# Where the two operands of a matmul begin: stationary tiles at 64 bytes, moving tiles at 192

## The chip, the cores and the metric

One core of a Trainium2 chip runs the kernel. The metric is the device time of one launch in microseconds, as the median of several runs. Lower is better.

## The reference

The input is q, k and v of 8 batches, 8 heads, 576 rows and a head size of 64. Each head computes a linear attention, its rows are normalized, and the result, as 4,608 rows of 512, passes through two dense layers with a GELU between them.

```python
kv = np.einsum('bhsd,bhse->bhde', k, v)
out = np.einsum('bhsd,bhde->bhse', q, kv)
rms = np.sqrt(np.mean(out * out, axis=-1, keepdims=True) + 1e-06)
x = (out / rms * g_norm)         # then transposed and reshaped to 4608 x 512
h = x @ w_in                     # 512 -> 2048
g = 0.5 * h * (1.0 + erf(h * inv_sqrt2))
return (g @ w_out)               # 2048 -> 512
```

## The kernel before

The 4,608 rows are cut into nine chunks of 512. The first two chunks (`PLAIN`) run both dense layers as plain matmuls (L665 for layer 1, L692 for layer 2, 512 columns each), while the other engines form sums of weight blocks and store them in DRAM. The other seven chunks, from `FAST` on, run each layer as seven block products instead of eight. These seven chunks are where the change is.

Every value is split into a high and a low part, and a product of two values is made of three matmuls: high with high, low with high, high with low. A matmul has a stationary operand, which is loaded into the array first (LDWEIGHTS, in the profile PEld), and a moving one, which then streams through. In these seven chunks each matmul has 128 stationary columns and 256 moving ones.

- Layer 1 (`product`, matmul at L554): the weights are stationary and the pieces of x are moving. It goes over eight parts j, each with seven products. A product of one key pair is six matmuls; two products share one place of weights, so twelve matmuls read the same place. The halves of the parts are interleaved by `parts_of_layer1`. Three matmuls per k block go through stationary high, low, high.
- Layer 2 (`Fast.matmuls`, matmul at L1241): the activations are stationary (`op`) and the weights are moving (`w`). It goes over 28 ticks (`TICKS`), of twelve matmuls each. The stationary operand goes high, high, low.

Between the parts of layer 1 stand other matmuls of the next chunk: the projections of q (L241), the fold of the sums of squares (L293) and the sums of keys and values (L188).

The weights come from DRAM in transfers of 512 KB through a ring of six places (`RING`, filled by `fetch`, released by `used`), or stay in SBUF for good (`keep` for four of layer 1; `kept_half` for nine of layer 2). A place is a tile of 4,096 bytes in each partition; those of the ring and of the kept weights have 256 bytes more (`EXTRA`), so that what lies in them may begin a little behind their start. `LINE` is 16 elements (64 bytes) and `AWAY` is three of them (192 bytes).

Before the change, all weights that come through the ring begin at `AWAY`, except those that `aligned` names, which begin at the place's start: the first of layer 2's ticks in each chunk, and three or four products of layer 1 in each chunk. In the first six chunks these follow a change of what TensorE works on (another layer, or L241, L293 or L188); in the last chunk three of them stand between other products of layer 1. The kept weights of both layers begin at `AWAY`. The other operand of each of these matmuls (pieces of x in layer 1, activations in layer 2) begins at a place's start.

The order of the instructions is that of the code; the pools hold every tile at a fixed place.

Of the kernel before, what the change touches and what calls it, by code (L numbers as in the profile page):

```python
# [9 lines left out]
F32R = mybir.dt.float32r  # L10
# [13 lines left out]
FAST = PLAIN  # L24
# [13 lines left out]
def linear_attn_rms_gelu_ffn(  # L38
# [18 lines left out]
    NT, DM = out.shape  # L57
    B, NP = kv_main.shape[:2]
# [5 lines left out]
    NCH = NT // CH  # L64
# [27 lines left out]
    LINE = 16  # L92
    AWAY = 3 * LINE
    KEPT_IN = [f"w_out{i}" for i in (4, 5, 6, 7)]
# [9 lines left out]
    def block_tile(name, dtype):  # L104
        return const.tile([P, 2 * DM + EXTRA.get(name, 0)], dtype, name=name)
# [69 lines left out]
    def rows(r):  # L175
        return slice(r * D, (r + 1) * D)
# [209 lines left out]
    kept = {}  # L386

    def reused(i, dtype=F32):

        if i not in kept:  # L390
            kept[i] = block_tile(f"w_in{i}", dtype)
        return kept[i][:, :2 * DM]
# [77 lines left out]
    TICKS = [(0, 0), (0, 1), (0, 2), (2, 0), (2, 1), (0, 3), (2, 2), (2, 3)]  # L470
# [19 lines left out]
    resident = {}  # L490
    queue = []
# [5 lines left out]
    ring = {}  # L497

    def fetch(n):

        if n < len(queue):
            key = queue[n][1]
            i = RING[n % len(RING)]
            reused(i, F32R)
            away = 0 if aligned(*queue[n]) else AWAY
            ring[n] = kept[i][:, away:away + 2 * DM]
            nc.sync.dma_start(out=ring[n].bitcast(F32), in_=products[key])

    def aligned(c, key):

        kind, j, k = key
        if kind == "out":
            return (j, k) == TICKS[0]
        if k:
            return False
        if c > FAST and c + 1 < NCH:
            return j in ((0, 1, 4, 7) if c + 2 < B else (0, 1, 4))
        return j in (0, 2, 3, 4)

    def operand(c, key):  # L520
        at = c, key
# [2 lines left out]
    def used(c, key):  # L524
        if (c, key) in place:
            n = place[c, key]
            ring.pop(n)
            fetch(n + len(RING))
# [5 lines left out]
        return name, block_tile(name, dtype)[:, :2 * DM]  # L534

    def keep(key):
        t = resident[key] = block_tile(KEPT_IN[key[1]], F32R)[:, AWAY:AWAY + 2 * DM]
        nc.sync.dma_start(out=t.bitcast(F32), in_=products[key])

    SETS = (("h0", "h1"), ("acc0", "acc1"), ("acc2", "acc3"))  # L540
# [242 lines left out]
    for d in range(0, 2 * D, BLK):  # L783
        h = d // D * D
        nc.gpsimd.tensor_tensor(
            out=fold[:, d:d + BLK], in0=ident[:, h:h + BLK], in1=ident[:, h + BLK:h + 2 * BLK],
# [24 lines left out]
    def column(n, t):  # L811
        return n_fold + 2 * ((n - 2) * NG + t)

    def sum_squares(n):
# [12 lines left out]
        out=half_g, in0=ps[:, :1], scalar1=0.5, scalar2=None, op0=ALU.mult  # L827
# [3 lines left out]
        out=sums[:, :P], lhsT=ones, rhs=eps, start=True, stop=False,  # L831
# [4 lines left out]
        out=root_g, in0=half_g, scalar1=D ** 0.5, scalar2=None, op0=ALU.mult  # L836
# [9 lines left out]
    for half in range(2):  # L846
# [6 lines left out]
        out=sums[:, :n_fold].rearrange("p (g b) -> p g b", g=2), lhsT=fold,  # L853
# [3 lines left out]
    for half in range(2):  # L857
        nc.scalar.activation(
            out=first.block((1, half)),
# [8 lines left out]
    for half in range(2):  # L868
# [3 lines left out]
            out=first.o_all[:, half], in0=first.ps.pop((0, half)), scalar=root_g, in1=bc,  # L872
            op0=ALU.mult, op1=ALU.mult,
        )
        n = 2 + half
        bc = bank(f"acc{n}")
        for t in range(NG):
            for h in range(2):
                at = column(n, t) + h
                nc.tensor.matmul(  # L880
                    out=bc[rows(h), t * P:(t + 1) * P],
# [173 lines left out]
    def later(c, i):  # L1055

        if i == 7:
            sums[c] = attn[c + 1].fold()
        if i in (5, 7):
            load_kv(c + 2, (i - 5) // 2)  # L1060
        if i == 9:
            attn[c + 2].load(0)
        if i == 10:
            attn[c + 2].load(1)
        if i in (5, 7):
            raw_out(6 + i // 7)
        if i == 15:
            place_kv(c + 2, range(NP))
        send()
        for n in {9: (0, 1), 14: (2, 3), 15: (4, 5)}.get(i, ()):  # L1070
            fetch(n)
        for n in {6: (0,), 9: (1,), 12: (2,), 14: (3,)}.get(i, ()):
            keep(RESIDENT[n])
# [43 lines left out]
    for s in range(PLAIN * NF):  # L1117
        c, i = divmod(s, NF)
# [5 lines left out]
        if c == 0:  # L1124
# [25 lines left out]
            for _ in range(2):  # L1150
                if i > 6 and RAW:
                    store_raw, j = RAW.pop(0)
# [8 lines left out]
        else:  # L1161
            spread_matmuls(c, i)
            g[s] = gelu(h.pop(s))
            nxt, k = attn[c + 1], SQUARES.index(i) if i in SQUARES else None
# [189 lines left out]
    for c in range(FAST, NCH):  # L1354
        at = attn[c]
# [3 lines left out]
        for j, second in parts_of_layer1():  # L1359
# [26 lines left out]
            if waiting and (last or (j, second) != (waiting[0], True)):  # L1386
                n = waiting.pop(0) // 2
# [65 lines left out]
```

## Time and profile before

| What | Value |
|---|---|
| Median of 3 runs | 775.71 us (775.59 to 778.14) |
| Span of the profiled execution | 774.5 us |
| What the two shortest runs lie above that span | 1.1 to 1.2 us |
| TensorE matmul (PE) busy | 767.6 us, 99% |
| TensorE weight load (PEld) busy | 726.5 us, 94% |
| VectorE (DVE) busy | 578.8 us, 75% |
| ScalarE (ACT) busy | 360.4 us, 47% |
| GpSimd (POOL) busy | 157.7 us, 20% |
| Packets of the main DMA queue | 87.9% of 16 engines' span |
| Mean granted TensorE clock | 0.999 |

The profile is of one execution, and its own time is given only as the span from the first to the last instruction; the time of a run also holds what lies around that. In the timeline a row is a number of like instructions in a row: its start, the time until the modelled end of the last one, the engine, the line, the operation, what it writes and reads, and how many there are. Matmuls overlap each other, so a row's own length is longer than what it adds; the start of one row to the start of the next is what the instructions took. Tile names are those of the places, which are used over and over: a piece of x can lie in a place called `w_in` or `s`.

### The profile page before, as it was taken

The page shows a single profiled execution, that of the slowest core. Times are in us where ns is not written, and L with a number is a line of the kernel's source. Part 1 is how long each engine was busy: PE and PEld are TensorE (multiplying, and loading weights), DVE is VectorE, ACT ScalarE, POOL GpSimd, SP SyncE. Part 2 cuts the span into 40 slices and gives each one's busy share as a digit, 9 for nine tenths or more (in the row PEclk, how much of TensorE's full clock was granted, in tenths as well). Part 3 has the DMA queues.
Part 4 walks back from the last instruction along what each step waited for, and adds up shares of the span by engine and source line. Part 5 has one row for each costly group of instructions (what it writes and reads, how often), then busy time and mean ns, then how long its engine had stood idle before and what let it go on. Part 6 is the DMA issues. An engine that isn't in the chain of part 4 may idle for free.

```text
span 774.5 us, 16764 instructions
## 1 busy us (share of the span) xinstructions
PE 767.6 (99%) x6598; PEld 726.5 (94%) x6598; DVE 578.8 (75%) x1057; ACT 360.4 (47%) x689; POOL 157.7 (20%) x141
## 2 busy tenths in 40 slices
PE   8999999999999999999999999999999999999998
PEld 6888888888899999999999999999999999999998
DVE  3999987899668974789477947694689568964683
ACT  3777645534363644364334724462436353632460
POOL 1000145423527000610043002500160016001100
PEclk9999999999999999999999999999999999999999
DMA  9997966797999999979998999989898989799974
GB/s 343 406 408 255 334 227 227 241 357 263 337 312 353 374 339 348 372 266 353 349 356 298 320 376 332 335 276 346 306 328 281 346 302 325 243 329 339 331 244 168
DMA packets 89602, 244.89 MB, mean 316 GB/s; under 512 B 8884, under 2 KB 30900, under 8 KB 89524
## 3 DMA queue, kind: packets, MB, share of 16 engines
q1 hardware_dynamic: 89520, 243.83, 87.9%
q8 instruction: 52, 0.85, 0.4%
q14 instruction: 26, 0.21, 0.1%
q10 hardware_dynamic: 4, 0.00, 0.0%
HBM read 207.09 MB, written 34.08 MB: 311 GB/s over the span
## 4 chain that ended last, share of the span: by engine, by line
PE 95%; DMA 2%; DVE 2%; ACT 0%; SPq 0%; issue 0%
PE acc L1241 23%; PE acc L554 22%; PE h L554 13%; PE acc L692 11%; PE h L665 11%; PE a L1241 10%; PE a L188 2%; PE a L241 1%; DMA kv_main<-kv_main 1%; PE h L655 1%; DMA w_in<-qT 1%; PE acc L241 1%; DVE x L1219 1%; PE acc L880 0%; PE a L293 0%; DVE x L1208 0%
## 5 line engine op out<-in xcount | busy, mean ns | idle before, releaser
L665 PE MATMUL h<-x,w_in 128*128 128x512 f32 x360 | 87.0, 390 | 0.0
L665 PEld LDWEIGHTS h<-x,w_in 128*128 128x128 f32 x360 | 67.3, 188 | 14.4 <-ACT w_in L641 0.3
L692 PE MATMUL acc<-w_out,gh 128*128 128x512 f32 x256 | 79.6, 392 | 0.0
L554 PE MATMUL acc<-w_in,w_in 128*128 128x256 f32 x480 | 64.7, 278 | 0.0
L554 PEld LDWEIGHTS acc<-w_in,w_in 128*128 128x128 f32 x480 | 59.1, 188 | 0.3 <-issue 0.2
L692 PEld LDWEIGHTS acc<-w_out,gh 128*128 128x128 f32 x256 | 47.5, 188 | 10.2 <-issue 0.3
L554 PE MATMUL acc<-x,w_in 128*128 128x256 f32 x390 | 52.8, 279 | 0.0
L545 DVE TENSOR_TENSOR gl<-acc,gh 128x256 f32<-128x256 f32 (+1 forms) x77 | 34.4, 446 | 24.2 <-ACT gh L567 18.5
L692 PE MATMUL acc<-w_out,gl 128*128 128x512 f32 x128 | 49.8, 389 | 0.0
L554 PEld LDWEIGHTS acc<-x,w_in 128*128 128x128 f32 x390 | 48.1, 188 | 1.0 <-issue 0.8
L678 ACT ACTIVATE gh<-h 128x512 fp32r<-128x512 f32 x32 | 19.2, 599 | 63.0 <-PE h L665 63.0
L1241 PE MATMUL acc<-w_in,w_in 128*128 128x256 f32 x372 | 46.7, 277 | 0.0
L567 ACT COPY gh<-h 128x256 f32<-128x256 f32 x21 | 7.8, 369 | 81.7 <-PE h L554 81.7
L1241 PEld LDWEIGHTS acc<-w_in,w_in 128*128 128x128 f32 x372 | 44.4, 188 | 0.0
L1208 POOL TENSOR_TENSOR w_in<-w_in,w_in 128x512 f32<-128x512 f32 x5 | 6.5, 1298 | 181.5 <-ACT w_in L586 181.5
L1241 PE MATMUL acc<-w_in,x 128*128 128x256 f32 x324 | 40.6, 277 | 0.0
L334 POOL TENSOR_TENSOR o<-o,sq 128x512 f32<-128x512 f32 x24 | 33.3, 1386 | 35.2 <-DVE sq L338 34.3
L586 ACT ACTIVATE w_in<-acc 128x512 f32<-128x512 f32 x32 | 19.2, 599 | 44.0 <-DVE acc L545 44.0
L554 PE MATMUL h<-w_in,w_in 128*128 128x256 f32 x288 | 38.7, 277 | 0.0
L1241 PEld LDWEIGHTS acc<-w_in,x 128*128 128x128 f32 x324 | 38.6, 188 | 0.1
L283 DVE TRANSPOSE_TENSOR_REDUCE part<-sq 128x16 f32<-128x512 f32 x33 | 23.4, 708 | 17.1 <-ACT sq L273 17.1
L554 PEld LDWEIGHTS h<-w_in,w_in 128*128 128x128 f32 x288 | 35.5, 188 | 0.0
(302 smaller groups left out, 1911.2 us busy)
## 6 DMA issues: line engine op xcount, KB each, us to landing
w_in<-products_in SPq DMA_DIRECT2D x168, 512.0 KB, 5.3
w_in<-products_out SPq DMA_DIRECT2D x133, 512.0 KB, 5.1
products_in<-w_in SPq DMA_DIRECT2D x40, 256.0 KB, 3.9
w_in<-w_in SPq DMA_DIRECT2D x16, 512.0 KB, 10.2
kv_main<-kv_main SPq DMA_DIRECT2D x16, 512.0 KB, 6.4
w_out<-w_out SPq DMA_DIRECT2D x16, 512.0 KB, 10.2
q<-qT SPq DMA_DIRECT2D x15, 512.0 KB, 6.5
products_out<-w_out SPq DMA_DIRECT2D x23, 256.0 KB, 3.9
```

Source lines behind the costliest of these rows:

```text
L188: nc.tensor.matmul(out=ps[r, n * D:(n + 1) * D], lhsT=k[:, r], rhs=v[:, r], start=(j == 0), stop=(j == NJ),)
L241: nc.tensor.matmul(out=ps[rows(h), p % 2 * HALF + a:p % 2 * HALF + e], lhsT=kv[b % 2][rows(half), p, h ^ half], rhs=q[rows(half), h, a:e], ...
L283: nc.vector.tensor_reduce(out=self.part[:, 2 * k[0] + k[1], :], in_=sq.rearrange("p (b d) -> p b d", d=BLK), op=ALU.add, axis=AX.X, apply_ ...
L334: eng.tensor_tensor(out=o, in0=o, in1=bc, op=ALU.mult)
L545: return eng.tensor_tensor(out=out, in0=x, in1=y, op=op)
L554: nc.tensor.matmul(out=out, lhsT=y, rhs=x[:, z, kb], start=first and kb + i == 0, stop=kb == 1 and i == 2, skip_group_check=True,)
L567: nc.scalar.copy(out=u[:, left], in_=a[:, left])
L586: nc.scalar.activation(out=grid(t)[:, :, j % 2], in_=ps.rearrange("p (a n) -> p a n", a=2), func=AF.Gelu)
L665: nc.tensor.matmul(out=h, lhsT=parts["in", i][:, w][:, p * P:(p + 1) * P], rhs=at.x[p][:, x], start=(m + p == 0), stop=(m == 2 and p == NP ...
L678: nc.scalar.activation(out=gh, in_=h, func=AF.Gelu)
L692: nc.tensor.matmul(out=ps, lhsT=x[:, ts], rhs=parts["out", i][:, w], start=(i == 0 and m == 0), stop=(m == 2 and (i == NF - 1 or (i, t) == ...
L1241: nc.tensor.matmul(out=self.bank[name][a][:, a * HALF:(a + 1) * HALF], lhsT=x[:, at], rhs=y, start=(k in (0, 2, 1) and n + p + m == 0 and ...
```

## The change

The weights of layer 1 now begin at `LINE`, 64 bytes into their places, both those of the ring and the four that are kept. The weights of layer 2 begin at `AWAY`, 192 bytes, all of them. The function `aligned` and its list are gone. No instruction is added, removed or moved, and the instructions, their order and their waits are the same on every engine; only starting addresses of operands in these places differ (of 2,436 matmuls and 179 transfers).

```diff
             i = RING[n % len(RING)]
             reused(i, F32R)
-            away = 0 if aligned(*queue[n]) else AWAY
-            ring[n] = kept[i][:, away:away + 2 * DM]
+            at = LINE if key[0] == "in" else AWAY
+            ring[n] = kept[i][:, at:at + 2 * DM]
             nc.sync.dma_start(out=ring[n].bitcast(F32), in_=products[key])
-
-    def aligned(c, key):
-
-        kind, j, k = key
-        if kind == "out":
-            return (j, k) == TICKS[0]
-        if k:
-            return False
-        if c > FAST and c + 1 < NCH:
-            return j in ((0, 1, 4, 7) if c + 2 < B else (0, 1, 4))
-        return j in (0, 2, 3, 4)
...
     def keep(key):
-        t = resident[key] = block_tile(KEPT_IN[key[1]], F32R)[:, AWAY:AWAY + 2 * DM]
+        t = resident[key] = block_tile(KEPT_IN[key[1]], F32R)[:, LINE:LINE + 2 * DM]
         nc.sync.dma_start(out=t.bitcast(F32), in_=products[key])
```

## The prediction

> **What bounds the kernel now.** I read the page's totals and its chain first, then the waits of PE, and then the timeline of PE, where the cost of a starting byte shows.
>
> ```profile
> span 774.5 us, 16764 instructions
> PE 767.6 (99%) x6598; PEld 726.5 (94%) x6598; DVE 578.8 (75%) x1057; ACT 360.4 (47%) x689; POOL 157.7 (20%) x141
> PEclk9999999999999999999999999999999999999999
> PE 95%; DMA 2%; DVE 2%; ACT 0%; SPq 0%; issue 0%
> ```
>
> PE is busy all the time, carries 95% of the chain that ended last, and has its full clock in every slice. The waits of PE, all there are that end at DMA or at another engine:
>
> ```profile
> PE a L188 <- DMA kv_main<-kv_main: 1.2, 2, 0.8
> PE h L772 <- DVE w_in L741: 1.1, 1, 1.1
> PE a L188 <- DMA w_out<-kv_main: 0.5, 2, 0.3
> PE h L818 <- ACT gl L807: 0.4, 1, 0.4
> PE acc L241 <- ACT kv L199: 0.3, 1, 0.3
> PE acc L1241 <- DVE x L1219: 0.2, 1, 0.2
> ```
>
> They are 3.7 us in all, and in the two lines that the change touches (L554 for layer 1, L1241 for layer 2) there is one, of 0.2 us. So time is lost or won only by the spacing of PE's own matmuls, and the busy times of the page, which are unions, don't show that. The timeline does: each product is 12 matmuls (6 where two products share half a place), and from one row's start to the next is what they took.
>
> I name a product by its two remainders modulo 256 bytes, counted from the start of a place (all places start alike, since each is 4,096 or 4,352 bytes and the built program puts them end to end; steps within an operand are multiples of 512 bytes). "Distance" is that of the moving operand minus that of the stationary one, in bytes. Before, layer 1 has +64 (moving 0, stationary 192), layer 2 has -64 (moving 192, stationary 0), and the products listed by `aligned` have 0. First the change from layer 1 to layer 2 in the first chunk of seven products: 250.31 is layer 1 at +64, 250.99 is the first tick of layer 2 at 0, the rest layer 2 at -64.
>
> ```profile
> 250.31 0.84 PE L554 MATMUL acc<-w_in,w_out 128*128 128x256 f32 x6
> 250.99 1.60 PE L1241 MATMUL acc<-w_in,w_in 128*128 128x256 f32 x12
> 252.43 1.54 PE L1241 MATMUL acc<-w_in,s 128*128 128x256 f32 x12
> 253.81 1.52 PE L1241 MATMUL acc<-r,x 128*128 128x256 f32 x12
> 255.17 2.88 PE L1241 MATMUL acc<-w_in,x 128*128 128x256 f32 x24
> ...
> 261.26 1.42 PE L1241 MATMUL acc<-w_out,x 128*128 128x256 f32 x10 [0.22 <-DVE x L1219]
> ```
>
> At +64 six matmuls take 0.68 (113 ns each). At distance 0 twelve take 1.44 (120 ns each). The next twelve, at -64, take 1.38, and then every twelve take 1.36 (113 ns). So both signs run at 113 ns once settled, distance 0 costs 0.08 us more for twelve, and settling afterwards costs 0.02.
>
> At -64 the settling is general. In layer 2 it also follows a block of other matmuls (L188) directly:
>
> ```profile
> 271.90 1.65 PE L1241 MATMUL acc<-w_in,x 128*128 128x256 f32 x12
> 273.38 0.84 PE L1241 MATMUL acc<-w_in,w_out 128*128 128x256 f32 x6
> ```
>
> These twelve take 1.48: 0.12 above 1.36, most of it the first gap after another kind of matmul. At +64 it isn't general. Around the start of the first chunk:
>
> ```profile
> 207.03 1.59 PE L554 MATMUL h<-x,w_in 128*128 128x256 f32 x12
> 208.47 1.52 PE L554 MATMUL h<-w_in,w_in 128*128 128x256 f32 x12
> 209.82 0.63 PE L692 MATMUL acc<-w_out,gh 128*128 128x512 f32 x2
> ...
> 212.57 1.58 PE L554 MATMUL acc<-x,w_in 128*128 128x256 f32 x12
> 213.98 1.58 PE L554 MATMUL acc<-w_in,w_in 128*128 128x256 f32 x12
> 215.40 1.57 PE L554 MATMUL h<-w_in,w_in 128*128 128x256 f32 x12
> 216.81 0.86 PE L554 MATMUL h<-w_in,w_out 128*128 128x256 f32 x6
> 217.61 1.10 PE L241 MATMUL a<-q,kv 64*64 64x192 f32 x24
> 218.63 1.69 PE L554 MATMUL acc<-x,w_in 128*128 128x256 f32 x12
> 220.16 0.50 PE L554 MATMUL acc<-w_in,w_in 128*128 128x256 f32 x3
> ```
>
> The product at 207.03 is at 0 (1.44) and the one at 208.47 at +64, settled (1.35). From 212.57 layer 1 runs at +64 straight after L692, with no product at 0 between, and it never settles: 1.41, 1.42, 1.41 for twelve, 118 ns a matmul, until L241 breaks it off. So +64 has a second, slower spacing, into which it falls when it starts in the wrong step, and a product at distance 0 brings it into the faster one. At -64 every start that the trace holds ended at 113.
>
> **The change, part by part.** No instruction is added, dropped or moved, and no wait changes. Of 4,704 matmuls in L554 and L1241, 2,040 move their stationary operand from 192 to 64, 312 (26 products) from 0 to 64, and 84 (7 products) their moving operand from 0 to 192; 179 transfers into these places land elsewhere by as much. All 4,704 then stand at -64. The settled products gain nothing: 1.36 stays 1.36. What goes are the 33 products at 0 and the slow stretch. The other rows that price them, each a start-to-start of twelve:
>
> ```profile
> 292.42 0.87 PE L554 MATMUL h<-x,w_in 128*128 128x256 f32 x6
> ...
> 293.85 1.52 PE L554 MATMUL h<-x,w_in 128*128 128x256 f32 x12
> ...
> 297.19 0.98 PE L554 MATMUL acc<-x,w_in 128*128 128x256 f32 x6
> ...
> 298.73 1.52 PE L554 MATMUL acc<-x,w_in 128*128 128x256 f32 x12
> ...
> 311.78 0.95 PE L554 MATMUL acc<-x,w_in 128*128 128x256 f32 x6
> ...
> 313.29 1.52 PE L554 MATMUL acc<-x,w_in 128*128 128x256 f32 x12
> ...
> 328.79 0.98 PE L554 MATMUL acc<-x,w_in 128*128 128x256 f32 x6
> ...
> 330.32 1.52 PE L554 MATMUL acc<-x,w_in 128*128 128x256 f32 x12
> ...
> 702.11 0.88 PE L554 MATMUL acc<-w_in,w_in 128*128 128x256 f32 x6
> ...
> 703.55 1.52 PE L554 MATMUL acc<-w_in,w_in 128*128 128x256 f32 x12
> ```
>
> 1. First tick of layer 2, in 7 chunks: 1.44 + 1.38 becomes 1.36 + 1.36 with a settling of 0.02 (that at 252.43 is the nearest row, and a change of layer still makes one odd pair): 0.08 each. In the first chunk PE then only waits longer at 261.26, where DVE's x is late. So 6 x 0.08 = 0.48.
> 2. First product of layer 1 behind layer 2, chunks two to seven: 1.43 (292.42 to 293.85) to 1.38: 6 x 0.05 = 0.30.
> 3. Behind the projections (L241), twice in the first chunk and once in each of the next five, 7 in all: 1.54 (297.19 to 298.73; 1.53 at 218.63) to 1.48, the price at 271.90: 7 x 0.06 = 0.42.
> 4. Behind the fold (L293), 6 times: 1.51 (311.78 to 313.29). It is 0.02 to 0.03 shorter than that behind L241, in its first gap, so the price after is 1.46: 6 x 0.05 = 0.30.
> 5. Behind the sums of keys (L188), 3 times: 1.53 (328.79 to 330.32) to 1.48, the same predecessor as at 271.90: 0.15.
> 6. In the last chunk three listed products stand with nothing before them but other products: 1.44 (702.11 to 703.55) to 1.36: 0.24.
> 7. In the first chunk: 1.44 at 207.03 to 1.38, and the slow stretch, 3 x 0.055 and half of one, less a settling of 0.02: 0.23.
>
> The sum is 2.12 us. Its bounds: if nothing had to settle, items 1 to 5 and 7 would give some 0.7 more, 2.8 in all; if each switch cost as much as a product at 0 does now, only items 6 and the slow stretch are left, 0.4. I take the middle terms because the two rows at -64 (252.43 and 271.90) are starts of just these kinds.
>
> What hides or takes back: DVE's chain at the start of layer 2. In the fifth chunk DVE ends the low part of an operand at 587.17, and the product that reads it begins at 587.24:
>
> ```profile
> 586.48 0.69 DVE L1219 TENSOR_TENSOR w_in<-w_in,w_in 128x512 fp32r<-128x512 f32 x1
> 587.24 1.52 PE L1241 MATMUL acc<-w_out,w_in 128*128 128x256 f32 x12
> ```
>
> The low part is the stationary operand of its third matmul, which comes two spacings later, at 587.47, with a weight load one spacing ahead of it, at about 587.36 (an estimate from the 0.113). So some 0.18 us are spare, and 0.08 of them are used up: no new wait, but not far from one. The transfers show no wait of PE in L554 or L1241. Their new landing place is priced by no row; now they land at 0 and at 192, and PE waits for neither, so I cost it at nothing. PE runs ahead by at most 0.4 us in a chunk, and since its release of a ring place starts the next transfer, the transfers move with it.
>
> **Against the rule.** The Trainium skill's page "SBUF — State Buffer", section "Who interferes with whom", gives PE two read ports, one for the moving operand and one for the weight load, which it calls independent, and says that PE never waits on anyone. By that the starting bytes of the two operands can't matter and the sum would be 0. The rows at 250.99 and 702.11 differ from it: 1.44 at distance 0 against 1.36, on the same engine with no wait.
>
> **The rivals.**
> - *The slow spacing catches layer 1.* Settling at -64 may belong to layer 2 (its stationary operands repeat, hi, hi, lo; layer 1's go hi, lo, hi) and not to the distance. Without the products at 0, layer 1 then falls into 118 ns after each switch. Price: 196 products of twelve x 0.055 = 10.8 us, less 1.6 for items 1 and 3 to 6: about 785, slower. It makes the kernel slower by 0.5% from about 110 of the 196 on (110 x 0.055 is the 3.9 us of that bound and the 2.1 of the sum). For it speaks 212.57 to 217.61; against it, that no start at -64 stayed slow, behind a product at 0, behind L188 or behind a stall.
> - *The residue isn't the cause.* Most listed products stand behind a switch, and what they cost could be the switch's. Then nothing changes: 775.7. Against it stand the three of the last chunk (1.44 behind an undisturbed 1.36), so this can hold for items 2 to 5 at most, which leaves 1.0 us: 774.7.
> - *Given back in waits.* If PE's lead meets DVE's low parts at every start of layer 2 and DVE can't move, items 1 and 2 return as waits, 0.8 us: 774.5. The one spare 0.18 above speaks against it.
>
> **How the numbers follow.** The profiled span is 774.5; the two close runs, 775.6 and 775.7, lie 1.1 to 1.2 above it, which is what lies around the span, and I apply the sum to the median: 775.7 - 2.1 = 773.6. A measurement of this kernel can tell about 0.5%, 3.9 us, from no change. Chances: the forecast (gain of 1.2 to 2.8) 0.74; waits or switches that take back more than that 0.13; the slow spacing in enough of layer 1 to be over 0.5% slower 0.08; a gain over 3.9 us, for which no row is known, 0.05. The likeliest alone reaches from 772.9 to 774.5; with the second case, up to no change, 8 in 10 lie from 772.6 to 775.9. Faster 0.05, same 0.87, slower 0.08.
>
> **What would show it.** In the timeline after: twelve matmuls at 1.36 at the first tick of layer 2 or 1.38 (item 1), 1.38 or less at the start of layer 1 (2), 1.48 behind L241 and L188 (3, 5), 1.36 throughout the last chunk (6), no product at 1.41 (7, and the slow rival). A longer wait of PE for DVE at the first chunk's layer 2, and none new elsewhere. Wrong it would be if products of layer 1 ran at 1.41 or 1.44 for long, or if ring transfers appeared among PE's waits.

## The result: slower by 1.1%

| | Before | After |
|---|---|---|
| Median | 775.65 us (775.47 to 778.14, 4 runs) | 784.09 us (783.77 to 785.64, 4 runs) |
| Ratio | | 1.0107 (95% interval 1.009 to 1.0123) |
| Span of the profiled execution | 774.5 us | 782.1 us |
| PE busy | 767.6 us | 776.6 us |

The page of the changed kernel, its totals and clock:

```profile
span 782.1 us, 16764 instructions
PE 776.6 (99%) x6598; PEld 735.7 (94%) x6598; DVE 578.6 (74%) x1057; ACT 359.8 (46%) x689; POOL 157.7 (20%) x141
PEclk9999999999999999999999999999999999999999
```

Its waits of PE are fewer than before, 2.3 us in all: these two, and two of 0.4 (for ACT) and 0.3 (in L241) as before. The one in layer 2 is gone:

```profile
PE h L761 <- DVE w_in L730: 1.1, 1, 1.1
PE a L188 <- DMA kv_main<-kv_main: 0.5, 1, 0.5
```

Neither the clock nor a wait is behind the loss. The same matmuls stand further apart. The timeline of PE in the second chunk of the seven (layer 1 is now L543, layer 2 L1230; a row of twelve lasts 1.52 at 113 ns and 1.58 at 118 ns, to the modelled end of its last matmul):

```profile
334.39 0.84 PE L543 MATMUL acc<-s,w_out 128*128 128x256 f32 x6
335.07 1.58 PE L1230 MATMUL acc<-w_in,w_in 128*128 128x256 f32 x12
336.49 1.58 PE L1230 MATMUL acc<-w_in,s 128*128 128x256 f32 x12
337.90 1.58 PE L1230 MATMUL acc<-r,w_out 128*128 128x256 f32 x12
...
373.24 1.58 PE L1230 MATMUL a<-w_out,w_in 128*128 128x256 f32 x12
374.65 0.87 PE L543 MATMUL h<-w_out,w_in 128*128 128x256 f32 x6
```

Layer 1 ends settled (0.68 for six, 113 ns each). Layer 2 starts straight behind it at 1.42 for twelve and is still at 1.41 in its last product: 118 ns each, to the end. This is the spacing that the kernel before shows only from 212.57 to 217.61, and there in layer 1.

What it costs is in a table of stretches: all of layer 2 in that chunk, and all of layer 1 in the last one, which is a plain stream of 336 matmuls. After, then the same stretches before:

```profile
335.07:374.65 39.58, 39.58 (x338) 1.00 0.91 332
701.09:740.67 39.58, 39.58 (x339) 1.00 0.93 322
```

```profile
335.76:373.94 38.18, 38.18 (x338) 1.00 0.92 337
694.57:732.95 38.38, 38.38 (x338) 1.00 0.92 336
```

Layer 2 takes 1.40 us longer in this chunk. The next four chunks are the same, and the five lose 7.0 us together. Layer 1 of the last chunk takes 1.20 longer. That is 8.2, against 7.6 us between the spans: the two plain chunks ended 0.6 us earlier in this execution, and what the other stretches gain and lose cancels out.

In the first chunk, layer 2 starts slow too, but doesn't stay so:

```profile
260.54 1.58 PE L1230 MATMUL acc<-w_out,x 128*128 128x256 f32 x12
261.96 4.24 PE L1230 MATMUL acc<-w_in,w_in 128*128 128x256 f32 x36
```

Its first eight products take 1.41 to 1.42 each. From 261.96 on, 36 matmuls end after 4.24, so they stand at 113 ns. In the product at 260.54, whose operand PE waited for before, the third matmul took 143 ns until the next one started, and soon after it the spacing is 113. So a stream can change its spacing on the way; that the late matmul was the cause isn't shown. These eight products take 11.31 us, and 11.53 before, with the wait.

The last chunk's layer 2 is the exception. It follows a layer 1 at 118 ns, and settles at 113:

```profile
739.96 0.87 PE L543 MATMUL acc<-w_in,w_out 128*128 128x256 f32 x6
740.67 1.54 PE L1230 MATMUL acc<-w_in,x 128*128 128x256 f32 x12
742.04 1.52 PE L1230 MATMUL acc<-w_in,s 128*128 128x256 f32 x12
```

So a distance of -64 has both spacings too. What stood ahead of the start is the difference that the rows show; the experiments test it.

### The profile page after: what moved, and what is told of

The parts are those of the page before. It is cut to its first block, busy times and chain, and to the rows that moved or that the text cites. A ratio compares the mean times of both kernels' runs of the same rounds, so it can differ in the third digit from the quotient of the medians.

```text
span 782.1 us, 16764 instructions
## 1 busy us (share of the span) xinstructions
PE 776.6 (99%) x6598; PEld 735.7 (94%) x6598; DVE 578.6 (74%) x1057; ACT 359.8 (46%) x689; POOL 157.7 (20%) x141
## 4 chain that ended last, share of the span: by engine, by line
PE 97%; DMA 2%; SPq 0%; DVE 0%; issue 0%
PE acc L1230 25%; PE acc L543 22%; PE h L543 13%; PE acc L681 11%; PE h L654 11%; PE a L1230 10%; PE a L188 2%; PE a L241 1%; DMA kv_main<-kv_main 1%; PE h L644 1%; DMA w_in<-qT 1%; PE acc L241 1%; PE acc L869 0%; PE a L293 0%; SPq L151 0%; DVE w L534 0%
## 5 line engine op out<-in xcount | busy, mean ns | idle before, releaser
L543 PE MATMUL acc<-w_in,w_in 128*128 128x256 f32 x480 | 65.1, 279 | 0.0
L543 PEld LDWEIGHTS acc<-w_in,w_in 128*128 128x128 f32 x480 | 59.4, 188 | 0.3 <-issue 0.2
L543 PE MATMUL acc<-x,w_in 128*128 128x256 f32 x390 | 52.5, 278 | 0.0
L543 PEld LDWEIGHTS acc<-x,w_in 128*128 128x128 f32 x390 | 47.8, 188 | 1.0 <-issue 0.8
L1230 PE MATMUL acc<-w_in,w_in 128*128 128x256 f32 x372 | 47.7, 280 | 0.0
L1230 PEld LDWEIGHTS acc<-w_in,w_in 128*128 128x128 f32 x372 | 45.3, 189 | 0.0
L1230 PE MATMUL acc<-w_in,x 128*128 128x256 f32 x324 | 41.5, 280 | 0.0
L1230 PEld LDWEIGHTS acc<-w_in,x 128*128 128x128 f32 x324 | 39.4, 189 | 0.1
L543 PE MATMUL h<-w_in,w_in 128*128 128x256 f32 x288 | 39.1, 278 | 0.0
L543 PEld LDWEIGHTS h<-w_in,w_in 128*128 128x128 f32 x288 | 35.8, 188 | 0.0
```

The costliest lines, as they stand in the source:

```text
L543: nc.tensor.matmul(out=out, lhsT=y, rhs=x[:, z, kb], start=first and kb + i == 0, stop=kb == 1 and i == 2, skip_group_check=True,)
L1230: nc.tensor.matmul(out=self.bank[name][a][:, a * HALF:(a + 1) * HALF], lhsT=x[:, at], rhs=y, start=(k in (0, 2, 1) and n + p + m == 0 and ...
```

## The experiments

"Listed" means the products that the old list put at 0. "Fast" and "slow" below are the spacings of 113 ns (1.36 for twelve) and 118 ns (1.41). Names such as `e2_list` are those of the runs.

**The first tick alone put back** (`e1_tick`). The changed kernel, with this edit:

```diff
-            at = LINE if key[0] == "in" else AWAY
+            at = LINE if key[0] == "in" else 0 if key[1:] == TICKS[0] else AWAY
```

> The changed kernel, but the first tick of layer 2 in each chunk has its weights at 0 again (7 products). Theory 1 (a stream of matmuls at a distance of 64 bytes either way has two lasting spacings, 113 and 118 ns, its first pairs decide which, and twelve matmuls at distance 0 always lead into 113): all of layer 2 runs at 113 (1.36 us for twelve), which takes back some 6.7 us of the 8.4, so about 777.4; layer 1 stays as in the changed kernel. Theory 2 (layer 2 is slow because layer 1's weights now lie at 64, by the distance both layers share or by where the transfers land): seven products change little, about 784.5.

Measured: 777.14 us, ratio to the kernel before 1.0013 (1.0004 to 1.0022). Seven products at 0 take back most of the loss. The timeline at the start of layer 2:

```profile
335.46 1.60 PE L1230 MATMUL acc<-w_in,w_in 128*128 128x256 f32 x12
336.90 1.54 PE L1230 MATMUL acc<-w_in,s 128*128 128x256 f32 x12
338.28 1.52 PE L1230 MATMUL acc<-r,w_out 128*128 128x256 f32 x12
```

1.44, then 1.38, then 1.36 to the end, as before the change, in all seven chunks. Theory 1 gave the time and the place; theory 2 (layer 1's bytes make layer 2 slow) falls.

**The whole list put back** (`e2_list`; the function `aligned` comes back with it, as it was), so that only layer 1's 64 in place of 192 is left of the change:

```diff
-            at = LINE if key[0] == "in" else AWAY
+            at = 0 if aligned(*queue[n]) else LINE if key[0] == "in" else AWAY
...
```

> The changed kernel with the whole old list at 0 again (33 products), so that against the kernel before only layer 1's other weights begin at 64 in place of 192. Theory 1: the sign of the distance is nothing of weight, everything settles at 113, about 775.7 (775.2 to 776.2). Theory 2: layer 2, or layer 1 too, still has rows of 1.41 for twelve; 780 to 785.

Measured: 783.78 us, ratio 1.0101 (1.0078 to 1.0124). Theory 1 missed. Layer 1 behind its listed products:

```profile
297.03 0.98 PE L554 MATMUL acc<-x,w_in 128*128 128x256 f32 x6
...
298.56 1.58 PE L554 MATMUL acc<-x,w_in 128*128 128x256 f32 x12
299.97 0.87 PE L554 MATMUL h<-s,w_in 128*128 128x256 f32 x6
```

The product at 0 (297.03 to 298.56) is followed by 1.41. All 2,040 unlisted matmuls of layer 1 are slow here, by a count of the trace's starts, and all of layer 2 is fast. So a product at 0 doesn't always lead into the fast spacing. When the stationary operand then moves on to 64, the stream is slow; when it moves to 192, as in the kernel before, the stream is fast.

**No list, the old 192** (`e3_nolist`). The kernel before, without the products at 0:

```diff
-            away = 0 if aligned(*queue[n]) else AWAY
+            away = AWAY
```

> The kernel before without the list: all weights of both layers at 192, so layer 1 at +64, layer 2 at -64, and no product at 0. Theory 1: long stretches at 1.41, in layer 1, in layer 2 or in both, 780 to 788. Theory 2 (the change's loss comes from the bytes at 64 or from both layers having one distance): 773.5, what was predicted for the change.

Measured: 782.21 us, ratio 1.0072 (1.0056 to 1.0089). So the products at 0 are worth something at the old bytes too: without them the kernel loses 6 us, though nothing lies at 64. Theory 1 holds. Two starts of layer 2 in this run, in the fourth chunk and in the fifth:

```profile
499.36 0.87 PE L554 MATMUL acc<-s,w_out 128*128 128x256 f32 x6
500.07 2.90 PE L1241 MATMUL acc<-w_in,w_out 128*128 128x256 f32 x24
502.81 1.41 PE L1241 MATMUL acc<-r,w_out 128*128 128x256 f32 x11
...
578.46 0.84 PE L554 MATMUL acc<-w_in,w_out 128*128 128x256 f32 x6
579.14 1.58 PE L1241 MATMUL acc<-w_in,w_in 128*128 128x256 f32 x12
580.55 1.58 PE L1241 MATMUL acc<-w_in,x 128*128 128x256 f32 x12
```

A slow layer 1 (0.71 for six) hands over to a fast layer 2 (2.74 for twenty-four), a fast one (0.68) to a slow one (1.41). The seven starts of layer 2 here all follow this rule, and so do the seven of the changed kernel and those of the next two runs: 28 of 28 starts of layer 2 at 192 without a product at 0, with layer 1 at 64 or at 192. It doesn't hold for the change from layer 2 to layer 1: there, at 192, fast follows fast and slow follows slow in this run.

**Layer 1's part of the list put back, layer 2 without** (`e4_listl1`). The changed kernel, with `aligned` back:

```diff
-            at = LINE if key[0] == "in" else AWAY
+            at = AWAY if key[0] == "out" else 0 if aligned(*queue[n]) else LINE
...
```

> The changed kernel with layer 1's part of the old list at 0 again (26 products), layer 2 all at 192. Theory 1: layer 1 is at 113 throughout, layer 2 starts straight behind a settled layer 1 and is at 118 in all seven chunks, the last one too (some 1.5 us lost there, 1.5 won in layer 1): 783.5 to 785. Theory 2 (layer 2 is slow because of layer 1's bytes): the same loss, but the last chunk's layer 2, at 113 in the changed kernel, stays at 113: 782.5.

Measured: 783.33 us, ratio 1.0087 (1.0072 to 1.0102). The time is near what theory 1 gave, for another reason: layer 1 is slow behind every listed product (as in the second run), and layer 2, without any product at 0, is fast in all seven chunks, by the rule just found.

```profile
336.13 0.87 PE L554 MATMUL acc<-s,w_out 128*128 128x256 f32 x6
336.83 1.54 PE L1241 MATMUL acc<-w_in,w_in 128*128 128x256 f32 x12
338.21 1.52 PE L1241 MATMUL acc<-w_in,s 128*128 128x256 f32 x12
```

A total that agrees can hide two errors that cancel; only the rows show it.

**One part of the change alone: the first tick at 192** (`e12_notick`), in the kernel before:

```diff
-            away = 0 if aligned(*queue[n]) else AWAY
+            away = 0 if key[0] == "in" and aligned(*queue[n]) else AWAY
```

> One part of the change alone: the kernel before with the first tick of layer 2 at 192 like the rest (7 products), layer 1 with its whole list and 192 as before. If layer 2 falls into 118 whenever it starts straight behind a layer 1 at 113: 6 chunks x 1.5 us plus 0.4 in the first, less 7 x 0.1, so about 784.2. If layer 2 starts well by itself when layer 1 lies at 192: 775.1.

Measured: 784.28 us, ratio 1.011 (1.0093 to 1.0127). Taking seven products out of distance 0 costs as much as the whole change. The other 172 transfers that the change moves lie here as they did before, so where they land isn't what makes layer 2 slow.

```profile
334.49 0.84 PE L554 MATMUL acc<-s,w_out 128*128 128x256 f32 x6
335.17 1.58 PE L1241 MATMUL acc<-w_in,w_in 128*128 128x256 f32 x12
336.58 1.58 PE L1241 MATMUL acc<-w_in,s 128*128 128x256 f32 x12
```

**What decides behind a product at 0.** Three runs (`e8_pad`, `e9_order`, `e10_mirror`), each one execution, ask why leaving it leads to fast in layer 2 (moving operand to 192) and to slow in layer 1 (stationary operand to 64), although the distance is -64 in both. The first moves all tiles by 64 bytes in the second run above (whole list, 64):

```diff
+    pad = const.tile([P, 16], F32, name="pad")
     kv = [const.tile([P, NP, 2, D], F32, name=f"kv{s}") for s in range(2)]
```

> The kernel e2_list (whole list at 0, layer 1's other weights at 64, which ran at 118 in all 2,040 matmuls) with 64 unused bytes ahead of all tiles, so that every operand's address moves by 64 and all distances stay. If only the distance of the two operands counts: no change, 783.8, layer 1 at 1.41 for twelve, layer 2 at 1.36. If it is the absolute remainder of an address (now the stationary tiles at 64 lie on a multiple of 256): layer 1 goes to 1.36, about 775.7.

Measured: 783.72 us, layer 1 at 1.41 as without the pad. A shift of both operands by 64 bytes plays no part.

The second gives layer 1 the operand order of layer 2, again in `e2_list`:

```diff
-            for i, (y, z) in enumerate(((hi, 0), (lo, 0), (hi, 1))):
+            for i, (y, z) in enumerate(((hi, 0), (hi, 1), (lo, 0))):
```

> The kernel e2_list with the three matmuls of layer 1 in the order in which layer 2 has them (stationary high, high, low in place of high, low, high). If the order of the operands is why a distance of -64 runs at 113 in layer 2 behind a product at 0 and at 118 in layer 1: layer 1 at 1.36, about 775.7. If not (the byte that moves at the end of the product at 0 decides: the moving operand's in layer 2, the stationary one's in layer 1): still 1.41, 783.8.

Measured: 785.47 us in one execution with a span of 783.7. Layer 1 is slow as in the run it is made from, and its part from 297.03 there and 298.75 here is the same, twelve at 1.41; the 1.7 us more were already there when the seven chunks began (208.0 against 206.3). The order isn't what makes layer 1 slow.

The third is the mirror image, in the kernel before: layer 2's weights leave 0 by 64.

```diff
-            away = 0 if aligned(*queue[n]) else AWAY
+            away = 0 if aligned(*queue[n]) else AWAY if key[0] == "in" else LINE
...
-            resident[key] = t[:, AWAY:AWAY + 2 * DM]
+            resident[key] = t[:, LINE:LINE + 2 * DM]
```

> The kernel before with layer 2's weights (but the first tick's) at 64 in place of 192, so that its moving operand leaves the remainder 0 by 64 and the distance becomes +64. If what counts is the step out of the product at 0 (192 leads into 113, 64 into 118, whichever operand takes it): all 2,268 matmuls of layer 2 behind a first tick at 118, about 785. If it is the sign of the distance in each layer apart, or layer 2 settles at 113 by itself: 775.7.

Measured: 785.63 us. Layer 2 behind its first tick:

```profile
336.45 1.60 PE L1241 MATMUL acc<-w_in,w_in 128*128 128x256 f32 x12
337.89 1.58 PE L1241 MATMUL acc<-w_in,s 128*128 128x256 f32 x12
339.30 1.57 PE L1241 MATMUL acc<-r,w_out 128*128 128x256 f32 x12
```

1.44, then 1.41 to 1.42 for all the rest. So in both layers 192 out of a product at 0 leads to fast and 64 to slow, whichever operand moves. The sign of the distance alone doesn't decide: +64 is fast in layer 1 and slow in layer 2, -64 the other way round.

**Without any product at 0 in layer 1: 192 in the listed products, 64 in the rest** (`e11_hand`). This is `e2_list` with another edit, in one execution.

```diff
-            at = 0 if aligned(*queue[n]) else LINE if key[0] == "in" else AWAY
+            listed = aligned(*queue[n])
+            at = (AWAY if listed else LINE) if key[0] == "in" else 0 if listed else AWAY
```

> The kernel e2_list with layer 1's listed products at 192 in place of 0 (all others of layer 1 at 64; first tick of layer 2 at 0). If the product at 0 is not needed to lead a stream and the step from 192 to 64 in mid-stream carries the spacing of 113 over: layer 1 at 1.36 wherever the listed product itself started at 113 (start of layer 1, behind the fold), about 777 to 779. If any step to 64 leads into 118, as that from 0 did: 1.41 in nearly all of layer 1, about 783.

Measured: 775.28 us, beside 775.74 for the kernel before: better than either reading. Layer 1 behind the projections, and behind the sums of keys:

```profile
297.33 0.87 PE L555 MATMUL acc<-w_in,w_in 128*128 128x256 f32 x6
298.03 1.52 PE L555 MATMUL acc<-x,w_in 128*128 128x256 f32 x12
...
328.85 0.87 PE L555 MATMUL acc<-w_in,w_in 128*128 128x256 f32 x6
329.56 1.58 PE L555 MATMUL acc<-x,w_in 128*128 128x256 f32 x12
```

Behind L241 the listed product is slow (0.70 for its second six, from 297.33), and the step to 64 makes the stream fast in six of the seven places. In the seventh, at 224.11, and in all three behind L188, the same slow product and the same step leave it slow. So two names, fast and slow, are not the whole state of a stream.

**A distance of 128** (`e6_128`). Both layers at `2 * LINE`, no list:

```diff
-    AWAY = 3 * LINE
+    AWAY = 2 * LINE
...
-            away = 0 if aligned(*queue[n]) else AWAY
+            away = AWAY
```

> The kernel before without the list and with 128 in place of 192 for the weights of both layers, so that the distance is 128 everywhere. By the theory that two lasting spacings belong to a distance of 64 alone, 128 has one: 113 throughout, about 773.5. Rival: 128 has two spacings as well (rows of 1.36 and of 1.41 for twelve), 779 to 786. Second rival: 128 bytes count as the same remainder, 120 throughout, 1.44 for twelve: some 31 us more, about 805.

Measured: 798.74 us, ratio 1.0295 (1.028 to 1.0309). It is between the two rivals, and none of the three readings holds: no stretch of either layer runs at 113.

```profile
339.42 1.58 PE L1241 MATMUL acc<-w_in,w_in 128*128 128x256 f32 x12
340.83 1.59 PE L1241 MATMUL acc<-w_in,s 128*128 128x256 f32 x12
342.26 1.59 PE L1241 MATMUL acc<-r,w_out 128*128 128x256 f32 x12
...
673.62 1.60 PE L1241 MATMUL acc<-w_in,w_in 128*128 128x256 f32 x12
675.06 1.60 PE L1241 MATMUL acc<-w_in,x 128*128 128x256 f32 x12
```

Here, too, there are two lasting spacings, though close to each other. Most stretches go on at 1.42 to 1.43 for twelve (119 ns). All of layer 2 in the sixth chunk, from 673.62 on, and layer 1 behind the fold in four chunks stay at 1.44 (120 ns), as a product at 0 does.

**A shorter list** (`e5_shortlist`). The run without a list shows which starts are fast by themselves at 192: those at the head of layer 1 behind a fast layer 2, and those behind the fold from the second chunk on. A shorter list in the kernel before:

```diff
-        if c > FAST and c + 1 < NCH:
-            return j in ((0, 1, 4, 7) if c + 2 < B else (0, 1, 4))
-        return j in (0, 2, 3, 4)
+        if c == FAST:
+            return j < 5
+        return c + 1 < NCH and j in ((1, 7) if c + 2 < B else (1,))
```

> The kernel before (layer 1 at 192, layer 2 at 192) with a list cut to the products that the run without a list showed to be needed: in the first chunk parts 0 to 4 (one more than before), in the next five the one behind the projections (L241) and, where there is one, the one behind the sums of keys (L188); none at the start of layer 1, behind the fold (L293) or in the last chunk; the first tick of layer 2 as before. 20 products at 0 in place of 33. By the theory that a stream keeps the spacing (113 or 118) into which its start has led it, and that the start depends on what stood ahead and on both remainders: all that was left out starts at 113 by itself, gain 6 x 0.06 + 5 x 0.06 + 3 x 0.08 + 0.1 = 1.0 us, so 774.6. If a start behind the fold needs the product at 0 after all (as in the first chunk it did), 114 to 174 matmuls a chunk run at 118: 0.5 to 0.8 us a chunk, 777 to 779.

Measured: 774.92 us, ratio 0.9989 (0.998 to 0.9999), 0.8 us below the kernel before; the interval only just leaves out 1. Every start that lost its product at 0 is fast by itself, as the rows of all chunks show. Behind the fold, without a product at 0, twelve take 1.44 (1.51 before), and the second six of them are settled (0.68):

```profile
311.56 0.93 PE L554 MATMUL acc<-x,w_in 128*128 128x256 f32 x6
312.32 0.84 PE L554 MATMUL acc<-w_in,w_in 128*128 128x256 f32 x6
313.00 1.18 PE L554 MATMUL acc<-x,w_in 128*128 128x256 f32 x9
```

## Why the prediction was wrong, by its steps

The forecast was 773.6 us; 784.09 was measured.

- **What bounds the kernel** was right: PE's own spacing, full clock, no waits that matter. So were the two lasting spacings and their sizes, but the prediction gave the slow one to +64 alone.
- **The step that failed** is "At -64 every start that the trace holds ended at 113", taken as a property of the distance: all of layer 2 was to start at 113. The starts that it rested on (252.43, 271.90, 261.26) followed a product at 0, L188 or a stall. The start that the change newly makes, layer 2 straight behind a layer 1 at 113, is in none of them. It is slow in all six chunks where it occurs in the changed kernel, and in all seven of the run that changes the first tick alone; in the first chunk of both, the stream turns fast at the product that DVE holds up.
- **Item 1** counted the first tick as 0.08 us to be won in each of six chunks, 0.48. Those products were what led layer 2 into the fast spacing: without them 1.40 us are lost in each of five chunks. This alone turns the forecast over: the first tick alone costs 784.28 - 775.74 = 8.5 us, the whole change 8.4, and the tick put back leaves 777.14.
- **Item 2** (start of layer 1 at 1.38): from 374.65 on, layer 1 is slow until L241, 1.41 for twelve, and so it is in all six chunks. At 192 such a start is fast behind a fast layer 2, as the run without a list shows; at 64 it was slow behind a fast layer 2 as well, in the run with the first tick put back.
- **Items 4 and 5** came out. Behind the fold (six of six places) and behind the sums of keys (three of three) layer 1 settled at 113 in the changed kernel, and the first twelve cost 1.46 and 1.48, as priced:

```profile
311.19 0.94 PE L543 MATMUL acc<-x,w_in 128*128 128x256 f32 x6
...
312.65 0.62 PE L543 MATMUL acc<-x,w_in 128*128 128x256 f32 x4
...
328.15 0.97 PE L543 MATMUL acc<-x,w_in 128*128 128x256 f32 x6
...
329.63 0.62 PE L543 MATMUL acc<-x,w_in 128*128 128x256 f32 x4
```

- **Items 3 and 7** came out in part or not at all. The price of item 3 was that of a start behind L188, and no row had one behind L241 at -64: there layer 1 settled in four of seven places only. Item 7 counted on a fast layer 1 at the start of the first chunk; it is slow there from the first product up to the fold. Rows of the first chunk's layer 1, then of the fifth chunk's behind L241, each as long as slow rows are:

```profile
213.45 1.58 PE L543 MATMUL acc<-w_in,w_in 128*128 128x256 f32 x12
214.87 1.58 PE L543 MATMUL h<-w_in,w_in 128*128 128x256 f32 x12
...
546.66 1.58 PE L543 MATMUL acc<-w_out,w_in 128*128 128x256 f32 x12
```

- **Item 6** was the clearest saving on paper: three products at 1.44 in a stream of 1.36. That stream is now slow from 701.09 to 740.67, 1.20 us lost. The three products at 0 weren't what kept it fast: the short list leaves them out and its layer 1 stays fast at 192. At 64 the start behind layer 2 is slow, and the stream with it, also where layer 2 ahead is fast (the run with the first tick put back, all 336 matmuls at 1.41 for twelve).
- **The rivals.** The first named the slow spacing, and its time (about 785) is near the measured one by luck: it put the loss into layer 1, where 1.2 of the 8.2 us are, and not into layer 2, where the other 7.0 are. It asked whether the operand order was behind it; the reordered run speaks against that. It got a chance of 0.08, because against it stood that no start at -64 stayed slow: the starts were counted and not sorted by what stood ahead of them.
- **The upper bound** of 2.8 us adds 0.7 to the sum without its terms. By the settling of 0.02 that the prediction read, the 30 starts of items 1 to 5 and 7 give 0.6. The failure doesn't turn on it.
- **Against the rule.** The Trainium skill's page "SBUF — State Buffer", section "Who interferes with whom", calls PE's two read ports independent. The runs differ from what the prediction drew from that: with the same instructions in the same order, the starting bytes alone move the kernel from 774.92 to 798.74. What joins the two operands no run shows.

What stays open: why 192 out of a product at 0 ends fast and 64 slow, why the change from layer 1 to layer 2 at 192 turns fast to slow and slow to fast, why layer 1 at 64 settles behind L241 in some places only, and what else a stream carries, since the same slow product went both ways in the run without products at 0 in layer 1. No run here took a finer step than 64 bytes, and the first matmuls of the starts weren't compared one by one.

## What to carry to other kernels

Before a start, a product or a tile that looks slow is taken out, ask what the stream behind it does without it: one product that cost 0.1 us a chunk kept 1.4 us a chunk away. When rows seem to show that a stream always settles, sort them by what stood directly ahead, and check that the new start is among them. For matmuls whose weights are loaded each time, try the starting bytes of both operands over whole kernels, and compare the start-to-start times by place and not the totals: two kernels here, 784.09 and 783.33, had nearly the same total, one with its layer 2 slow and the other with its layer 1.

## What the hardware showed that was not expected

- A stream of matmuls of 128 stationary and 256 moving columns, with a weight load each, kept one of two spacings at a distance of 64 bytes, 113 or 118 ns, for up to 336 matmuls (38 to 40 us), with the same operands' places in both; which of them followed from its start, but in the first chunk of the changed kernel it turned from slow to fast on the way. At the same remainder it ran at 120 ns, and at a distance of 128 bytes at 119 or 120.
- Moving both operands by the same 64 bytes changed nothing (783.72 us in one execution against 783.78). What counted was where they lie against each other, and against the places of the product ahead.
